# Order and time of the first loads of a convolution that runs beside an MLP: tap rows stored early, inputs in order of need

## Chip, cores, metric

One NeuronCore of one Trainium2 chip. Times are device microseconds (us) of one launch. Most executions of one kernel agree within 0.3%.

## The reference

Forward and backward of a block that adds two branches on a layer-normed input: a causal long convolution (with a short four-tap shift convolution of `k` ahead of it) and a gated MLP. Cut to what matters here:

```python
def _A_ref(q, k, v, shift_k, ssm_k, ssm_D):            # convolution branch
    k_shift = sum of four shifted copies of k, each times a column of shift_k
    kv = k_shift * v
    y = irfft(rfft(kv) * rfft(ssm_k)) + kv * ssm_D
    return q * y
def _B_ref(x, W_gate, W_up, W_down):                   # MLP branch
    h = relu(x @ W_gate) * (x @ W_up)
    return h @ W_down
return x + _A_ref(xn, ...) + _B_ref(xn, ...)           # and all gradients (vjp)
```

bf16, 2048 rows, width 1024, MLP width 3584. On the chip the convolution is done by small matmuls and VectorE transposes, in eight groups of 128 channels, threaded between the MLP's large matmuls.

## The kernel before

TensorE works through the MLP's first phase in groups of eight matmuls: two "gate" groups, two "up" groups, two "ps_h" groups, and so on. A generator `steps()` puts the convolution's work between them. A clock of the program counts 1730 per group; the convolution starts when it reaches `A_START`, and each `yield n` gives the MLP another n.

```python
    def loads_1(self, gi):                       # filter hn, gradient gt, bias sD
        ...
        for ch in range(2):
            self.load(hn[...], self.ssm_k[...])  # runs of 32 bf16 values
        self.load_time(gt, self.g, cg)           # two transfers
        self.load(sD[:], self.ssm_D[cg].partition_broadcast(P))
    def loads_2(self, st):                       # kp: four transfers; vt: two
        ...
    def load_taps(self, st):                     # tap rows, broadcast to 128 partitions
        skb = st["skb"] = self.sm.tile([P, 4, 1, P], BF16, name="skb")
        self.load(skb..., self.sk_d[4 * gi:4 * gi + 4, :]...partition_broadcast(P))
    def steps(self):
        sk_t = self.shift_rows()                 # transpose on TensorE, copy on ScalarE
        self.pin = True
        nx = self.loads_1(0)                     # hn, gt, sD
        self.loads_2(nx)                         # kp, vt
        yield 5000
        self.load(self.sk_d, sk_t[:])            # tap rows stored to DRAM
        yield 5000
        self.load_taps(nx)                       # ... and loaded again as skb
        yield 7000
        self.load_xn(nx)
        ...
        self.begin(nx)                           # first tap product: ksh = kp * skb
A_START = 80_000
```

All these transfers, and the MLP's stores and weight loads, are issued by SyncE, one after the other. VectorE carries the convolution's tap products and transposes and also empties the MLP's PSUM tiles (`ru <- ru, ps_u`); the MLP has four PSUM tiles (`bufs=4`).

## Time and profile before

| kernel before | |
|---|---|
| median, first runs | 1915.82 us (1914.72 to 1916.49) |
| profiled execution | 1911.9 us on the core, 1913.69 us as timed |
| TensorE busy | 1879.4 us of it |
| VectorE's longest wait near the start of the convolution | 8.29 us, on skb |
| TensorE's waits there | 3.21 and 1.67 us |
| TensorE's clock just after the first wait | 0.50 |

Read it from the engine that sets the end: TensorE is busy nearly always, so a microsecond is gained only where TensorE stands or runs at a lowered clock. The lines of the profile are in the prediction. One caution: the trace of before holds 15217 matmul records. Some are missing, and the many "issue" waits of 0.2 us are the holes that they leave. The busy share (98% before) must not be read as an effect.

### The profile page before, as it was taken

How to read it: one execution, taken by the hardware profiler on the slowest of the kernel's cores; microseconds unless marked ns; L12 is line 12 of the kernel's file. 1: busy time of each engine (PE TensorE's matmuls, PEld its weight loads, DVE VectorE, ACT ScalarE, POOL GpSimd, SP SyncE). 2: the span in 40 equal slices, each digit the busy share in tenths (PEclk: the TensorE clock that was granted, in tenths of full speed). 3: DMA queues.
4: the chain of work that ended last, by engine and by line, in shares of the span. 5: the costliest groups of instructions: out<-in, count | busy, mean ns of one | idle time of the engine just before them, and what ended most of it. 6: DMA issues, size and time to landing. Idle time of an engine off the chain costs nothing.

```text
span 1911.9 us, 35799 instructions
## 1 busy us (share of the span) xinstructions
PE 1879.4 (98%) x15217; PEld 872.8 (46%) x15447; DVE 909.8 (48%) x1355; ACT 618.3 (32%) x858; POOL 15.0 (1%) x37
## 2 busy tenths in 40 slices
PE   9989999999999999999999999999999999999999
PEld 4434444444444444444444444444444544444444
DVE  6656777777777764553454454400222232222222
ACT  5645345345345445344344354321000000000000
POOL 1000000000000000000000000000000000000000
PEclk9999999999999999999999999999999999999999
DMA  9887679977577774566563633394999965544553
GB/s 251 249 187 167 154 198 195 201 199 167 135 202 154 218 221 112 141 149 208 133 168 99 171 100 124 104 283 143 254 248 243 230 153 121 122 122 121 121 122 72
DMA packets 692641, 323.14 MB, mean 169 GB/s; under 512 B 524024, under 2 KB 663040, under 8 KB 692480
## 3 DMA queue, kind: packets, MB, share of 16 engines
q1 hardware_dynamic: 681984, 299.99, 63.5%
q10 hardware_dynamic: 9216, 16.65, 2.9%
q0 software_dynamic: 1280, 4.20, 0.6%
q8 instruction: 120, 1.97, 0.4%
q14 instruction: 41, 0.34, 0.1%
HBM read 143.79 MB, written 95.44 MB: 125 GB/s over the span
## 4 chain that ended last, share of the span: by engine, by line
PE 95%; DMA 2%; issue 1%; SPq 1%; DVE 1%; ACT 0%; DVEq 0%
PE ps_x L1319 20%; PE ps_w L1092 19%; PE ps_o L1250 10%; PE ps_u L835 9%; PE ps_h L835 9%; PE ps_g L835 9%; PE ps_d L1092 9%; PE ps L72 6%; PE ps_d L1105 1%; SPq L88 1%; PE ps_w L1105 1%; DMA wu<-in_B_W_up_dram 1%; DMA wg<-in_B_W_gate_dram 1%; PE ps_r L1280 0%; DVE flp L302 0%
## 5 line engine op out<-in xcount | busy, mean ns | idle before, releaser
L1092 PE MATMUL ps_w<-ugs,xn_nat 128*128 128x512 bf16 x1673 | 375.5, 379 | 5.7 <-issue 4.1
L835 PEld LDWEIGHTS <-xnT 128*128 128x128 bf16 x1792 | 170.9, 98 | 216.4 <-issue 17.6
L1092 PEld LDWEIGHTS <-xn_nat 128*128 128x128 bf16 x1728 | 164.5, 98 | 200.6 <-issue 7.6
L835 PE MATMUL ps_g<-wg,xnT 128*128 128x512 bf16 x869 | 205.2, 382 | 6.9 <-DVE ru L939 3.2
L835 PE MATMUL ps_u<-wu,xnT 128*128 128x512 bf16 x869 | 205.5, 381 | 3.0 <-issue 1.3
L835 PE MATMUL ps_h<-wdT,goT 128*128 128x512 bf16 x861 | 202.1, 379 | 2.6 <-issue 1.3
L1337 ACT ACTIVATE w<-xn,m 128x512 f32<-128x512 bf16 x32 | 24.3, 807 | 553.0 <-issue 317.2
L1319 PE MATMUL ps_x<-wuT,guT 128*128 128x512 bf16 x878 | 197.5, 379 | 1.0
L1319 PE MATMUL ps_x<-wgT,ggT 128*128 128x512 bf16 x878 | 197.3, 379 | 0.9
L1250 PE MATMUL ps_o<-wd,hT 128*128 128x512 bf16 (+1 forms) x879 | 186.7, 372 | 0.9
L1092 PE MATMUL ps_d<-g_nat,hs 128*128 128x512 bf16 x741 | 167.4, 379 | 3.2 <-issue 2.7
L1319 PEld LDWEIGHTS <-guT 128*128 128x128 bf16 x896 | 87.7, 98 | 105.7
L1319 PEld LDWEIGHTS <-ggT 128*128 128x128 bf16 x896 | 87.6, 98 | 105.5
L302 DVE STREAM_TRANSPOSE flp<-C 128x1024 f32<-128x1024 f32 x48 | 90.1, 1930 | 91.9 <-ACT C L76 91.9
L1250 PEld LDWEIGHTS <-hT 128*128 128x128 bf16 x896 | 87.7, 98 | 100.0
L835 PEld LDWEIGHTS <-goT 128*128 128x128 bf16 x896 | 84.9, 98 | 104.6 <-issue 5.7
L939 DVE SCALAR_TENSOR_TENSOR ru<-ru,ps_u 128x512 bf16<-128x512 bf16 x112 | 76.5, 683 | 107.8 <-issue 45.2
L1008 ACT CAST gh<-ps_h 128x512 bf16<-128x512 f32 x112 | 65.4, 584 | 172.3 <-PE ps_h L835 162.0
L1196 ACT CAST wi<-ps_w 128x512 bf16<-128x512 f32 x108 | 63.7, 590 | 162.9 <-PE ps_w L1092 154.0
L76 ACT CAST C<-ps 128x1024 bf16<-128x1024 f32 x96 | 92.5, 1015 | 71.0 <-PE ps L72 69.8
L1092 PEld LDWEIGHTS <-hs 128*128 128x128 bf16 x768 | 72.3, 98 | 89.6 <-issue 5.9
L1321 DVE CUSTOM_DVE_ANT_0 gx<-ps_x,gy 128x512 f32<-128x512 f32 x32 | 22.1, 691 | 187.1 <-PE ps_x L1319 185.1
(160 smaller groups left out, 1495.3 us busy)
## 6 DMA issues: line engine op xcount, KB each, us to landing
ug_d<-ru SPq DMA_DIRECT2D x112, 256.0 KB, 3.1
ugs<-ug_d SPq DMA_DIRECT2D x112, 256.0 KB, 5.3
wg<-in_B_W_gate_dram SPq DMA_DIRECT2D x56, 256.0 KB, 4.1
wu<-in_B_W_up_dram SPq DMA_DIRECT2D x56, 256.0 KB, 5.2
h_d<-ht SPq DMA_DIRECT2D x112, 128.0 KB, 2.4
hs<-h_d SPq DMA_DIRECT2D x56, 256.0 KB, 5.2
out_dram<-wi SPq DMA_DIRECT2D x56, 256.0 KB, 2.3
gt<-in_grad_out_dram SPq DMA_DIRECT2D x32, 256.0 KB, 4.0
```

The lines of the kernel that those rows point to most:

```text
L72: self.pri.pin(self.nc.tensor.matmul(out, lhsT=lhsT, rhs=rhs, start=start, stop=stop))
L76: self.pri.pin(self.nc.scalar.copy(out=out, in_=in_))
L302: self.pri.pin(self.nc.vector.transpose(out=df[:, c0:c0 + 32, :], in_=sf[:, c0:c0 + 32, :]))
L835: self.pri.pin(self.nc.tensor.matmul(ps[:], lhsT=xT[:, kt * P:(kt + 1) * P], rhs=w(kt), start=(kt == 0), stop=(kt == self.DT - 1)), always ...
L939: self.pri.pin(nc.vector.scalar_tensor_tensor(out=ru[s][:, 1, :], in0=ru[s][:, 0, :], scalar=0.0, in1=ps[:], op0=ALU.is_gt, op1=ALU.mult))
L1008: self.pri.pin(nc.scalar.copy(out=gh[:], in_=ps[:]))
L1092: self.pri.pin(self.nc.tensor.matmul(ps[:], lhsT=lhsT(st), rhs=rhs(st), start=(st == 0), stop=(st == self.ST - 1)))
L1105: self.pri.pin(self.nc.tensor.matmul(ps[i][:], lhsT=lhsT(i, st), rhs=rhs(i, st), start=(st == 0), stop=(st == self.ST - 1)))
L1196: self.pri.pin(nc.scalar.copy(out=wo[0][:, d, :], in_=ps[:]))
L1250: nc.tensor.matmul(ps, lhsT=hT[:, kt, :], rhs=self.wd[:, kt, oc], start=(kt == 0), stop=(kt == self.FT - 1))
L1319: nc.tensor.matmul(ps, lhsT=T[:, kt, :], rhs=W[:, kt, oc], start=(i == 0), stop=(i == n - 1))
L1337: nc.scalar.activation(out=w[:, oc], in_=xn[:, oc], func=ACT.Identity, scale=m[:, 7:8], bias=m[:, 6:7])
```

## The change

Its intent: the tap rows are made, stored and thus ready long before the convolution starts, and the first group's inputs are loaded in the order in which they are needed, with the MLP's stores let in between. The arithmetic starts at the same place (97,000 on the program's clock in both). Core of the diff:

```diff
-        nx = self.loads_1(0)
-        self.loads_2(nx)
-        yield 5000
+        yield 10000
         self.load(self.sk_d, sk_t[:])
-        yield 5000
+        yield 25000
+        nx = self.load_filter(0)      # hn
+        yield 3400
+        self.load_k(nx)               # kp
         self.load_taps(nx)            # skb
-        yield 7000
+        yield 3400
+        self.load_g(nx)               # gt, sD
+        yield 3400
+        self.load_v(nx)               # vt
+        yield 6800
         self.load_xn(nx)
...
-A_START = 80_000
+A_START = 45_000
```

(cut: `loads_1` and `loads_2` are split into `load_filter`, `load_g`, `load_k`, `load_v`; the other groups call them in the old order.)

More of the change, by code (lines that the diff above doesn't have):

```diff
@@ L245, in ttile, with load_filter @@
         return self.ts.tile([P, 19, P], BF16, name=name, tag="ts")
-    def loads_1(self, gi):
+    def load_filter(self, gi):
         cg = slice(gi * P, (gi + 1) * P)
@@ L252, in loads_1, with load_g @@
             self.load(hn[64 * ch:64 * ch + 64], self.ssm_k[c0:c0 + 64, :].rearrange("c (q n) -> q c n", n=NB1))
-        gt = self.ld.tile([P, 16, P], BF16, name="gt")
-        self.load_time(gt, self.g, cg)
-        sD = self.sm.tile([P, P], BF16, name="sD")
-        self.load(sD[:], self.ssm_D[cg].partition_broadcast(P))
-        return dict(gi=gi, cg=cg, hn=hn, gt=gt, sD=sD)
+        return dict(gi=gi, cg=cg, hn=hn)
+    def load_g(self, st):
+        gt = st["gt"] = self.ld.tile([P, 16, P], BF16, name="gt")
+        self.load_time(gt, self.g, st["cg"])
+        sD = st["sD"] = self.sm.tile([P, P], BF16, name="sD")
+        self.load(sD[:], self.ssm_D[st["cg"]].partition_broadcast(P))
+    def loads_1(self, gi):
+        st = self.load_filter(gi)
+        self.load_g(st)
+        return st
     def load_xn(self, st):
@@ L264, in gate_grad, with load_k, load_v, loads_2 @@
         self.tt(st["gt"][:], st["gt"][:], st["xt"][:], ALU.mult)
-    def loads_2(self, st):
-        nc, cg = self.nc, st["cg"]
-        kp = self.lng.tile([P, 19, P], BF16, name="kp")
+    def load_k(self, st):
+        nc = self.nc
+        kp = st["kp"] = self.lng.tile([P, 19, P], BF16, name="kp")
         self.pri.now()
         nc.gpsimd.memset(kp[0:1, 0:3, :], 0.0)
-        kv = self.tview(self.k, cg)
-        self.load_time(kp[:, 3:19, :], self.k, cg)
+        kv = self.tview(self.k, st["cg"])
+        self.load_time(kp[:, 3:19, :], self.k, st["cg"])
         self.load(kp[64:P, 0:3, :], kv[0, :, 13:16, :])
         self.load(kp[1:64, 0:3, :], kv[1, 0:63, 13:16, :])
-        vt = self.lng.tile([P, 16, P], BF16, name="vt")
-        self.load_time(vt, self.v, cg)
-        st["kp"], st["vt"] = kp, vt
+    def load_v(self, st):
+        vt = st["vt"] = self.lng.tile([P, 16, P], BF16, name="vt")
+        self.load_time(vt, self.v, st["cg"])
+    def loads_2(self, st):
+        self.load_k(st)
+        self.load_v(st)
     def load_taps(self, st):
```

## The prediction

> **What bounds the kernel now.** I read the page first: busy shares and the chain that ended last.
>
> ```profile
> PE 1879.4 (98%) x15217; PEld 872.8 (46%) x15447; DVE 909.8 (48%) x1355; ACT 618.3 (32%) x858; POOL 15.0 (1%) x37
> ...
> PE 95%; DMA 2%; issue 1%; SPq 1%; DVE 1%; ACT 0%; DVEq 0%
> ```
>
> TensorE carries the run: busy 98% of 1911.9 us, and 95% of the last chain. A change that only moves loads and one small store can gain no more than TensorE loses to waiting and to a lowered clock at the place concerned. So the second view is TensorE's waits over the whole span (us in total, times, longest):
>
> ```profile
> PE ps_w L1092 <- issue: 4.1, 26, 0.2
> PE ps_g L835 <- DVE ru L939: 3.2, 1, 3.2
> ...
> PE ps L72 <- DVE flp L302: 1.7, 1, 1.7
> ```
>
> Two single waits stand out, 3.2 us on VectorE's evacuation of an "up" product and 1.7 us on a VectorE transpose of the convolution. All others are 1.5 us or less, or many waits of 0.2 us. The third view, TensorE in order of time (start, duration), puts both in one place, just where the convolution branch begins:
>
> ```profile
> 115.62 3.63 PE L835 MATMUL ps_h<-wdT,goT 128*128 128x512 bf16 x15
> 119.08 1.89 PE L835 MATMUL ps_g<-wg,xnT 128*128 128x512 bf16 x8
> 124.18 3.57 PE L835 MATMUL ps_g<-wg,xnT 128*128 128x512 bf16 x8 [3.21 <-DVE ru L939]
> 127.55 4.79 PE L835 MATMUL ps_u<-wu,xnT 128*128 128x512 bf16 x16
> 132.17 1.89 PE L835 MATMUL ps_h<-wdT,goT 128*128 128x512 bf16 x7
> 135.73 0.75 PE L72 MATMUL ps<-flp,FW 64*32 64x128 bf16 x64 [1.67 <-DVE flp L302]
> ```
>
> The first line is the yardstick: two groups of eight matmuls from 115.62 to 119.08, 1.73 us a group. After the 3.21 us gap one group takes 3.37 us from start to start and the next two 4.62 instead of 3.46. The view by stretches shows why (the granted clock is the third number from the end, then come the DMA share and GB/s):
>
> ```profile
> 121.00:124.20 3.20, 0.02 (x1) 0.02 (x1) 1.86 (x3) 0.60 (x1) 0.00 (x0) 0.83 1.17 178
> 124.20:127.50 3.30, 3.30 (x8) 1.11 (x8) 3.26 (x6) 0.00 (x0) 0.00 (x0) 0.50 1.12 237
> 127.50:132.00 4.50, 4.50 (x17) 1.81 (x16) 4.47 (x5) 0.60 (x1) 0.00 (x0) 0.73 0.62 177
> ```
>
> The granted clock is 0.50 just after the gap and 0.73 on average over the next 4.5 us. TensorE counts as busy here, so the busy share hides this loss. The last view is VectorE in order of time, then the queue of SyncE, which issues the transfers:
>
> ```profile
> 113.59 0.43 DVE L941 TENSOR_TENSOR ht<-ru 128x512 bf16<-128x512 bf16 x1
> 122.31 1.23 DVE L80 TENSOR_TENSOR ksh<-kp,skb 128x2048 bf16<-128x2048 bf16 x1 [8.29 <-DMA skb<-sk_d]
> 123.45 0.68 DVE L939 SCALAR_TENSOR_TENSOR ru<-ru,ps_u 128x512 bf16<-128x512 bf16 x1
> ```
> ```profile
> 99.43 4.78 SPq L88 DMA_DIRECT2D hn<-in_A_ssm_k_dram  x2
> ...
> 113.69 1.31 SPq L88 DMA_DIRECT2D vt<-in_A_v_dram  x2
> 115.10 0.71 SPq L1013 DMA_DIRECT2D ug_d<-ru  x1
> 115.91 0.56 SPq L88 DMA_DIRECT2D sk_d<-sk_t  x1
> ...
> 119.13 0.33 SPq L88 DMA_DIRECT2D skb<-sk_d  x1
> ```
>
> VectorE stands 8.29 us before the first tap product, which needs the broadcast tap row skb. Behind it in VectorE's queue waits the evacuation of an up group that TensorE had finished at about 115.15. The MLP has four PSUM buffers; that unread group, two ps_h groups and one ps_g group fill them, so the second gate group can't start at 120.81 and starts at 124.18, as the evacuation at 123.45 ends. And skb is late because the burst of first-group inputs holds SyncE from 99.43 to 115.00: the row copy sk_t was ready at 96.0 (ScalarE's copy began at 95.76 and took 0.25), its store was issued only at 115.91, its load at 119.13, and skb was there at 122.31.
>
> **What the Trainium skill says.**
> - "PSUM — Partial Sum Buffer", Engine vs sequencer instructions: the queues of VectorE and ScalarE are strict FIFO. The trace agrees: the evacuation, ready at 115.15, ran 1.14 us after the tap product began, not before.
> - "TensorE: Matmul & The Clock Gate", Part 1: an idle window of about 3.4 us halves TensorE's clock, about 3.4 us of sustained work restores it, and a 512-column matmul then takes 426.7 ns start to start rather than 215.7. The trace agrees closely: 3.37 us for 8 is 421 ns, against 1.73 / 8 = 216 ns; a gap of 3.21 us was enough.
> - "DMA: Bandwidth & Descriptors", Anatomy of one DMA: a semaphore wait of a transfer is spent on the issuing sequencer, before dispatch. So a load that reads a just-stored tensor holds the queue behind it. The trace has 0.9 us of such a wait of SyncE on sk_d; most of the delay was the queue itself.
> - The same page, Why small descriptors are slow: a fixed overhead per packet. Filter hn goes in runs of 64 bytes (32 bf16 values); its stretch from about 104 to 105.5 shows the 16 DMA engines full at some 145 GB/s, so hn is the dear input.
>
> **The change, part by part.** Nothing is taken away: same loads, same store, same arithmetic.
>
> 1. Start and length of the preamble: before 80,000 + 5,000 + 5,000 + 7,000 = 97,000 on the program's step clock; after 45,000 + 10,000 + 25,000 + 3,400 x 3 + 6,800 = 97,000. The convolution's arithmetic enters at the same place between the MLP's matmuls.
>
> 2. Tap rows: the transpose (0.23 us on TensorE) and its copy (0.25 us on ScalarE) move some 35 us earlier, and the store of 8 KB some 45 us or more earlier, to about 75 us, when SyncE has room. Cost unchanged. The wait for this store drops out of skb's path.
>
> 3. skb: now directly after kp. hn keeps its place (issue 99.43 to 104.2). kp follows two steps (3.4 us) later, with one or two stores between: about 105 to 110 (4.52 us of issue in the old trace, an upper figure, since it queued behind hn). Then skb, 0.33 us, and 122.31 - 119.13 = 3.2 us to landing: about 113.5. VectorE is free for the tap product at 114.02. The 8.29 us wait should be gone or down to one or two.
>
> 4. What TensorE gains. The old walk against full speed, start to start: first gate group 5.10 instead of 1.73, lost 3.37 (the gap); second gate group 3.37, lost 1.64; two up groups 4.62 instead of 3.46, lost 1.16; ps_h group 3.56 instead of 1.73, lost 1.83 (the transpose). Sum **8.0 us**. At full speed TensorE comes to the flp matmuls at 119.08 + 5 x 1.73 = 127.73, not 135.73.
>
> 5. What VectorE then allows. Its chain to the second transpose in the old trace ran with no gap after the stall. In the new one, tap product, evacuation, ht and second product end by about 117.5; then the first "ru x gh" product must wait for ScalarE's gh, ready at 117.56 + 0.58 = 118.14 as before. From that product's start to the end of the second transpose the old trace took 135.68 - 125.64 = 10.04 us, so at best the transpose ends at 118.18 + 10.04 = 128.2, and TensorE waits 0.5 us there. Gain left: **7.5 us**.
>
> 6. What the new order can give back. sD, needed by the bias addition right after that product (about 118.9), was third in line and is now after hn, kp, skb and gt. Adding the old issue times from 99.43: hn 4.78, kp 4.52, skb 0.33, gt 3.61, sD 1.17 is 14.4; with some 2 us of stores and one transposed weight load (1.40) it is issued at about 117 and lands near 120 if queues stay as full as before. They should be emptier, as the burst is spread, so I charge half of that 1.1 us delay, 0.6 us, all on the path since VectorE has no slack by step 5.
>
> Sum 7.5 - 0.6 = 6.9 us; the rest of the span has no other part in the change, so 1915.8 - 6.9 = **1908.9 us**, 0.36% less.
>
> **Rivals.**
> A. Another input takes skb's place. The DMA engines are full nearly throughout from 99 to 119 us, and kp comes behind hn; if kp, skb or sD land 3 us late, TensorE waits 2 to 3 us at the transpose, though with a shorter gap the clock should not fall. For it: the full engines. Against it: kp moves ahead of gt and sD, 4.8 us of issue. Time: 1910.5 to 1912.
> B. VectorE as the local bound: the stall only hides VectorE's backlog, and later hand-overs (the gate product, the next transposes) slip too. For it: VectorE runs with hardly a gap from 122.31 to 141.27. Against it: half of that is catching up, and it idles 3.75 us right after. Time: about 1911.
> C. Full gain, with the transpose in time and weight loads and stores no longer stuck behind the burst: 1907.5.
> D. The wait was hidden anyway, or the stores between the loads hold SyncE while they wait for VectorE (4.1 us at the longest in the old trace) and so delay kp as much as the burst delayed skb: 1914 to 1917. Against it: the last chain is nearly all TensorE, and later loads would have to have been the true limit.
>
> **Range and chances.** C and the main line together have most of the weight, A and B about a third, D little. Run to run the old kernel moved by under 2 us. Range 1906.8 to 1913. The whole loss at the place is 8.0 us, 0.4%, so over 2% (38 us) either way would need something I can't see: faster 0.005, same 0.985, slower 0.01.
>
> **What would show it.** Right: sk_d stored before 80 us; tap product ksh starting at 114 to 116 with no long wait on skb; no TensorE wait on ru L939; clock 1.00 in the stretch 120 to 132 us; flp matmuls at 127.7 to 130 us; later phases like the old ones, shifted by about 7 us. Wrong: a wait of ksh on kp or of the bias addition on sD over 2 us; a wait on flp above 1.67 us; the shift shrinking again at the next weight loads; a new gap before 115 us.

## The result

| | before | after |
|---|---|---|
| median of the same rounds | 1916.15 us (1914.72 to 1917.26, 4 runs) | 1906.98 us (1905.80 to 1908.47, 4 runs) |
| ratio, with 95% interval | | 0.9953 (0.9936 to 0.9970) |
| profiled span | 1911.9 us | 1904.1 us |

The gain is clear of noise, 9 us or 0.5%; against the 2% mark it is "same". The time is inside the predicted range, but only 0.2 us above its lower end of 1906.8.

Two of TensorE's longest waits in the whole run after the change (a third, of 1.5 us in two parts, is at the very start, in the layer norm, and is 0.2 us in r_after below); the wait on the evacuation of `ps_u` is gone, that on the transpose is down from 1.7 to 0.5 us:

```profile
PE ps_warm L899 <- POOL warm L896: 1.5, 1, 1.5
PE ps L72 <- DVE flp L314: 0.5, 1, 0.5
```

TensorE after, in order of time (start, duration; lines of the program have moved by 17, so L835 is now L852):

```profile
115.76 3.63 PE L852 MATMUL ps_h<-wdT,goT 128*128 128x512 bf16 x16
119.22 3.62 PE L852 MATMUL ps_g<-wg,xnT 128*128 128x512 bf16 x16
122.67 3.62 PE L852 MATMUL ps_u<-wu,xnT 128*128 128x512 bf16 x16
126.13 1.89 PE L852 MATMUL ps_h<-wdT,goT 128*128 128x512 bf16 x8
128.53 0.75 PE L72 MATMUL ps<-flp,FW 64*32 64x128 bf16 x64 [0.51 <-DVE flp L314]
```

From the start of the ps_h groups to the flp matmuls it was 135.73 - 115.62 = 20.11 us and is 128.53 - 115.76 = 12.77 us. I call this stretch the walk. It is 7.34 us shorter. The clock, in the view by stretches (third number from the end), stays at 1.00 where it was 0.83, 0.50 and 0.73:

```profile
121.00:124.20 3.20, 3.20 (x17) 1.43 (x16) 3.17 (x4) 1.19 (x2) 0.00 (x0) 1.00 1.17 226
124.20:127.50 3.30, 3.30 (x17) 1.53 (x16) 3.27 (x4) 0.00 (x0) 0.00 (x0) 1.00 1.18 240
127.50:132.00 4.50, 3.99 (x80) 1.91 (x79) 4.47 (x6) 3.10 (x4) 0.00 (x0) 1.00 0.71 189
```

VectorE after: the tap product waits 0.93 us for skb instead of 8.29, and everything behind it comes earlier.

```profile
115.08 1.23 DVE L80 TENSOR_TENSOR ksh<-kp,skb 128x2048 bf16<-128x2048 bf16 x1 [0.93 <-DMA skb<-sk_d]
...
118.42 0.69 DVE L1026 TENSOR_TENSOR ru<-ru,gh 128x1024 bf16<-128x1024 bf16 x1
...
126.55 1.93 DVE L314 STREAM_TRANSPOSE flp<-B 128x1024 f32<-128x1024 f32 x1
```

The queue of SyncE after: the store of the tap rows 49 us earlier, skb 7 us earlier, one MLP store (ug_d) let in behind hn.

```profile
66.68 0.55 SPq L88 DMA_DIRECT2D sk_d<-sk_t  x1
...
99.11 5.61 SPq L88 DMA_DIRECT2D hn<-in_A_ssm_k_dram  x2
104.81 2.52 SPq L1030 DMA_DIRECT2D ug_d<-ru  x1
107.38 4.59 SPq L88 DMA_DIRECT2D kp<-in_A_k_dram  x4
112.02 0.37 SPq L88 DMA_DIRECT2D skb<-sk_d  x1
```

I also compared the starts of the same-numbered VectorE evacuations in the two traces. The new kernel is 0.1 to 0.4 us late until 113 us, 7.2 us ahead from then until 230 us, and 7.8 us ahead at the end. So the place accounts for nearly all of it; another 0.6 us comes at weight loads near 240 and 390 us.

### The profile page after: what moved, and what is told of

Read it like the earlier page. It is cut to its first block, busy times and chain, and to the rows that moved or that the text cites. A ratio compares the mean times of both kernels' runs of the same rounds, so it can differ in the third digit from the quotient of the medians. Undisturbed runs are those within 1.5% of the kernel's fastest.

```text
span 1904.1 us, 36029 instructions
## 1 busy us (share of the span) xinstructions
PE 1895.0 (100%) x15447; PEld 871.9 (46%) x15447; DVE 910.1 (48%) x1355; ACT 618.2 (32%) x858; POOL 15.0 (1%) x37
## 4 chain that ended last, share of the span: by engine, by line
PE 97%; DVE 1%; DMA 1%; issue 0%; SPq 0%; ACT 0%; DVEq 0%; ACTq 0%
PE ps_x L1336 20%; PE ps_w L1109 20%; PE ps_o L1267 10%; PE ps_h L852 10%; PE ps_u L852 10%; PE ps_g L852 9%; PE ps_d L1109 9%; PE ps L72 6%; PE ps_d L1122 1%; PE ps_w L1122 1%; DMA wg<-in_B_W_gate_dram 0%; PE ps_r L1297 0%; DMA wu<-in_B_W_up_dram 0%; SPq L88 0%; DVE ru L956 0%
## 5 line engine op out<-in xcount | busy, mean ns | idle before, releaser
L1109 PE MATMUL ps_w<-ugs,xn_nat 128*128 128x512 bf16 x1728 | 383.3, 379 | 0.0
L852 PEld LDWEIGHTS <-xnT 128*128 128x128 bf16 x1792 | 170.3, 98 | 209.8 <-issue 9.1
L852 PE MATMUL ps_g<-wg,xnT 128*128 128x512 bf16 x896 | 206.3, 379 | 1.5 <-ACT xnT L887 0.4
L852 PE MATMUL ps_u<-wu,xnT 128*128 128x512 bf16 x896 | 206.9, 379 | 0.0
L852 PE MATMUL ps_h<-wdT,goT 128*128 128x512 bf16 x896 | 205.6, 379 | 0.0
L1109 PE MATMUL ps_d<-g_nat,hs 128*128 128x512 bf16 x768 | 172.1, 379 | 0.0
L1336 PEld LDWEIGHTS <-ggT 128*128 128x128 bf16 x896 | 87.7, 98 | 105.5
L852 PEld LDWEIGHTS <-goT 128*128 128x128 bf16 x896 | 85.0, 98 | 104.7 <-issue 5.8
```

The lines of the kernel that those rows point to most:

```text
L852: self.pri.pin(self.nc.tensor.matmul(ps[:], lhsT=xT[:, kt * P:(kt + 1) * P], rhs=w(kt), start=(kt == 0), stop=(kt == self.DT - 1)), always ...
L1109: self.pri.pin(self.nc.tensor.matmul(ps[:], lhsT=lhsT(st), rhs=rhs(st), start=(st == 0), stop=(st == self.ST - 1)))
L1336: nc.tensor.matmul(ps, lhsT=T[:, kt, :], rhs=W[:, kt, oc], start=(i == 0), stop=(i == n - 1))
```

## The experiments

Eleven kernels ran: seven built on the changed kernel, two on the kernel before, and these two again as they are. All gave right results. "Flp less ksh" is the time from the start of the first tap product to the flp matmuls. The ratio is against the kernel before, whose medians were 1915.48 us (first four rows), 1915.39 us (next four) and 1916.02 us (last three); the first two profiles lead the table.

| kernel | ksh starts | flp matmuls | flp less ksh | walk | median us | ratio (95% interval) |
|---|---|---|---|---|---|---|
| before, first profile | 122.31 | 135.73 | 13.42 | 20.11 | | 1 |
| after, first profile | 115.08 | 128.53 | 13.45 | 12.77 | 1906.98 | 0.9953 (0.9936 to 0.9970) |
| r_after | 115.42 | 128.87 | 13.45 | 12.73 | 1906.90 | 0.9957 (0.9944 to 0.9969) |
| e5_filler | 123.42 | 136.80 | 13.38 | 20.99 | 1916.78 | 1.0009 (0.9996 to 1.0023) |
| e1_store_early | 122.97 | 136.38 | 13.41 | 20.62 | 1914.60 | 0.9999 (0.9986 to 1.0012) |
| e4_burst | 114.82 | 128.43 | 13.61 | 12.67 | 1906.22 | 0.9955 (0.9942 to 0.9967) |
| e2_taps_first | 118.78 | 132.18 | 13.40 | 15.64 | 1910.67 | 0.9974 (0.9961 to 0.9988) |
| e3_store_late | 115.88 | 129.31 | 13.43 | 13.70 | 1908.65 | 0.9962 (0.9950 to 0.9975) |
| e6_skb_ahead | 115.77 | 129.20 | 13.43 | 13.43 | 1907.50 | 0.9958 (0.9943 to 0.9973) |
| e7_flip_sooner | 115.85 | 128.09 | 12.24 | 12.19 | 1907.33 | 0.9954 (0.9942 to 0.9967) |
| r_before | 123.74 | 137.15 | 13.41 | 21.06 | 1915.29 | 1.0002 (0.9987 to 1.0018) |
| e9_burst_flip | 114.69 | 128.15 | 13.46 | 12.19 | 1906.66 | 0.9951 (0.9939 to 0.9964) |
| e8_begin_later | 125.96 | 139.21 | 13.25 | (other order) | 1912.46 | 0.9976 (0.9964 to 0.9989) |

**My theory after the two traces:** the flp matmuls come when VectorE's chain from ksh to the second transpose is done, and ksh starts when its last input lands; so only the landing of skb (and kp) counts. Rivals: the lowered clock is a loss of its own; the hour of the store matters; the MLP's stores held behind the burst matter.

**r_after: the changed kernel again.**

> The changed kernel again, for its time beside the others of this call and to see which gains away from the place repeat. The walk is the time on TensorE from the start of the two ps_h groups (115.62 us before, 115.76 after) to the first flp matmuls (135.73, 128.53): 20.11 us before, 12.77 after. Expected: walk 12.7 to 12.9, time 7 to 9.5 us below the kernel before. In the first two traces the shift grew by another 0.65 us at weight loads near 240 and 390 us; if that is chance of the transfers it will be another value here.

Measured: walk 12.73, ratio 0.9957. The gain near 390 us came again, but at 530 us the kernel lost about 1 us at weight loads, so in this trace it ends 6.9 us ahead of before. What happens away from the place moves by a microsecond from run to run and isn't the change's.

**e5_filler: fill TensorE's gap, leave the rest as before.**

```diff
                 ru[s] = self.e2_tile("ru")
+                if n == 2 and s == 5:
+                    junk = self.fill_ps.tile([P, 2, 512], F32, name="ps_junk", tag="aps")
+                    for _ in range(15):
+                        matmul(junk[:, 0], lhsT=xT[s][:, 0:P], rhs=wg(0), start=True, stop=True)
                 ps = self.ps_tile("ps_g")
```

(cut: the matmul call is shortened, and one line that lends the filler a PSUM tile of the convolution is left out.)

> Kernel before with 15 idle-filling matmuls (15 x 0.216 = 3.24 us) between the first and the second gate group of that step, just where TensorE stood 3.21 us; their result is read by nobody. Loads, stores and VectorE unchanged. Theory of the prediction, in which the lowered clock is a loss of its own (1.64 + 1.16 us of the 8.0): the gap is filled, the clock stays at 1.00 and the flp matmuls come 2.8 us earlier, walk about 17.3. Rival, the VectorE chain: VectorE ran without a gap from 122.31 to 135.68, so the flp matmuls can't come sooner; TensorE gets to them earlier and waits 1.67 + 2.8 = 4.5 us there instead of 1.67; walk 20.1, time as before.

TensorE in order of time with the filler:

```profile
121.00 3.40 PE L934 MATMUL ps_junk<-wg,xnT 128*128 128x512 bf16 x15
125.30 1.89 PE L835 MATMUL ps_g<-wg,xnT 128*128 128x512 bf16 x8 [0.90 <-DVE ru L944]
127.02 3.62 PE L835 MATMUL ps_u<-wu,xnT 128*128 128x512 bf16 x16
130.47 1.89 PE L835 MATMUL ps_h<-wdT,goT 128*128 128x512 bf16 x8
136.80 1.05 PE L72 MATMUL ps<-flp,FW 64*32 64x128 bf16 x64 [4.44 <-DVE flp L302]
137.79 2.48 PE L835 MATMUL ps_h<-wdT,goT 128*128 128x512 bf16 x6
```

Up to the flp matmuls the clock held: eight gate matmuls take 127.02 - 125.30 = 1.72 us, not 3.37. Yet the flp matmuls came no sooner. The wait for the transpose grew from 1.67 to 4.44 us, flp less ksh is 13.38 as ever, and the time didn't fall. So up to the flp matmuls the lowered clock had cost nothing: it ran beside VectorE's backlog. But the filler did not do away with it. After the wait of 4.44 us the granted clock was 0.50 from 136.45 to 139.86 us (in the trace of before it was 1.00 there), and six ps_h matmuls took 2.48 us. By my estimate that is 1.5 us lost, half of the 3.06 us in which TensorE was at work. The whole time, 1.0009, contains this loss and a longer stall, so it does not show what a restored clock is worth; the unchanged flp less ksh does. The skb wait was 9.21 us here, 0.9 longer than in the first trace of before, which explains the walk of 20.99; the expected 20.1 took the wait for fixed.

**e1_store_early: only the store of the tap rows early; inputs in the old order and burst, skb behind them.**

```diff
         yield 25000
-        nx = self.load_filter(0)
-        ... (kp, skb, gt, sD, vt with yields between)
+        nx = self.loads_1(0)
+        self.loads_2(nx)
+        yield 10000
+        self.load_taps(nx)
+        yield 7000
```

> Changed kernel, but the first group's inputs in the old order and in one burst, and skb loaded at its old place behind them; only the transpose and the store of the tap rows stay early. Theory (the queue order is what made skb late): skb is issued at about 117.5 instead of 119.13 and lands at about 120.7, ksh begins 1.6 us earlier than before, and with 13.37 us from ksh to the end of the second transpose the walk is about 18.4: gain 1.7 us. Rival (the late store is the cause): ksh no longer waits more than 1 us, walk 12.8, gain 7.

VectorE and SyncE of this kernel:

```profile
122.97 1.22 DVE L80 TENSOR_TENSOR ksh<-kp,skb 128x2048 bf16<-128x2048 bf16 x1 [8.81 <-DMA skb<-sk_d]
```
```profile
118.09 0.60 SPq L88 DMA_DIRECT2D skb<-sk_d  x1
```

No gain at all: less than the 1.7 us I expected, and nothing of the rival's 7. skb is issued 1 us earlier than before but takes 122.97 - 118.09 = 4.9 us until VectorE can use it, where it took 3.2 us when SyncE had stood waiting for the store. My reading is that what had been issued ahead of it still had to move, whether SyncE waited or not. The packet records in the traces bear this out. Four stores of the MLP, 768 packets of 1024 bytes, were issued between the burst and skb. When skb was issued, 64 packets of this size had started here and 592 in the trace of before; the 768th of this size started at 120.12 and at 119.78 us, and skb was there 2.8 and 2.5 us after that. The early store by itself is worth nothing.

**e4_burst: new order, but no stores between.**

```diff
         nx = self.load_filter(0)
-        yield 3400
         self.load_k(nx)
         self.load_taps(nx)
-        yield 3400
         self.load_g(nx)
-        yield 3400
         self.load_v(nx)
-        yield 6800
+        yield 17000
```

> Changed kernel with the new order of need (hn, kp, skb, gt, sD, v) but in one burst, with no stores between. Theory (only skb and kp in time matter): skb is issued at about 110, ksh starts at about 114, walk 12.7 to 13, gain 7 to 9 as the changed kernel. Rival (the stores held behind the burst matter): buffers of ru or ht come free late, a new wait of 1 us or more, walk 14 or more.

Measured: ksh at 114.82, walk 12.67, ratio 0.9955: the whole gain. The stores between the loads, a part of the change, do nothing for the time here; if anything kp and skb come 0.3 us sooner without them. Flp less ksh is 13.61, the longest of all: ksh was so early that VectorE's chain then waited for the product with `gh`, as the prediction's fifth step has it.

**e2_taps_first: skb first of all, the others in the old order and burst.**

```diff
-        nx = self.load_filter(0)
-        ... (kp, skb, gt, sD, vt with yields between)
+        nx = dict(gi=0)
+        self.load_taps(nx)
+        nx.update(self.loads_1(0))
+        self.loads_2(nx)
+        yield 17000
```

> Changed kernel with skb loaded first of all, ahead of hn, and the other inputs in the old order (hn, gt, sD, kp, v) and one burst. So skb is out of the question and kp, issued last but one, is the last thing ksh needs. From the first runs: the flp matmuls start 13.4 us after ksh starts, in every kernel. Theory (order of need matters, kp takes skb's place): kp's issue ends near 114, its last piece lands at about 117 to 118, ksh starts there, walk 14.7 to 16, gain 4 to 6 us. Rival (skb alone mattered): ksh starts by 115, walk 12.7 to 13, full gain.

```profile
118.78 1.23 DVE L80 TENSOR_TENSOR ksh<-kp,skb 128x2048 bf16<-128x2048 bf16 x1 [3.84 <-DMA kp<-in_A_k_dram]
```

A little over half the gain. With skb out of the question, kp takes its place: ksh starts 2.24 us after the ps_h groups (116.54), in the changed kernel 0.68 us before them. TensorE had no gap on `ps_u` any more; it waited 3.4 us on the transpose and its clock stayed at 1.00. So both halves of "order of need" count: skb ahead, and kp ahead of gt and sD.

**e3_store_late: new order and spread, the store of the tap rows late.**

```diff
-A_START = 45_000
+A_START = 80_000
...
-        yield 10000
-        self.load(self.sk_d, sk_t[:])
-        yield 25000
         nx = self.load_filter(0)
         yield 3400
+        self.load(self.sk_d, sk_t[:])
         self.load_k(nx)
```

> Changed kernel with the transpose and the store of the tap rows back at their late time: the store is issued just before kp's loads, skb after them; all else as in the changed kernel. Theory (the place of skb in the queue is the cause, not the hour of the store): the store lands while kp's loads are being issued (over 4 us), skb is issued at about 112 to 113, ksh starts at 115 to 116, walk 12.7 to 13.7, gain 6 to 9. Rival (the early store is needed): SyncE stands some 3 us before skb, ksh starts at 118 or later, walk 16 or more.

Measured: skb issued at 112.65 with no wait ahead of it, ksh at 115.88, walk 13.70, ratio 0.9962. The walk just reaches the end of what I had expected, 0.9 us more than the changed kernel's; the store now sits in the queue ahead of kp (0.56 us at 108.76), which may be part of that. Nor is 0.9 us far from chance: e7_flip_sooner below has the loads of the changed kernel, and its ksh came 0.6 us later in the walk. So the early store is worth at most some 1 us, the order 6 us or more.

**e6_skb_ahead: new kernel, skb ahead of hn.**

```diff
-        yield 25000
+        yield 22000
+        nx = dict(gi=0)
+        self.load_taps(nx)
+        yield 3000
-        nx = self.load_filter(0)
+        nx.update(self.load_filter(0))
         yield 3400
         self.load_k(nx)
-        self.load_taps(nx)
```

> Changed kernel with skb loaded between its store and hn, so that only kp is left to wait for. Theory (in the changed kernel VectorE's chain starts at the first product with gh, 118.2 to 118.4, so the 0.9 us wait for skb costs next to nothing): ksh starts near 114, walk 12.5 to 12.8, no time clear of noise against the changed kernel. Rival: each us of ksh's wait costs a us; walk 11.9.

A miss. In this schedule a transposed weight load (1.32 us at 106.37) went ahead of kp, kp landed at 115.77 and ksh waited 1.60 us for it. Walk 13.43, 0.7 longer than the changed kernel's; the time can't tell them apart. It didn't test whether an earlier ksh would still gain; e4_burst and e9_burst_flip did.

**e7_flip_sooner: one tap operation of the first group moved behind the transposes on VectorE.**

```diff
             yield None, self.both(lambda: self.add_D(st), tk)
             yield None, tk
-            yield None, tk
+            if gi:
+                yield None, tk
...
             yield None, flH
             yield None, flH
+            yield None, tk
             yield None, tk
             yield f2H, tk
```

> Changed kernel with one of the seven tap operations of the first group (1.23 us) moved from before to behind the two transposes on VectorE. Theory (the remaining 0.5 us wait of TensorE is VectorE's chain): the wait is gone, walk 12.3, and nothing waits in its place. Rival: the displaced operation delays the gate product and a wait of 0.5 us or more comes at the gt matmuls. Either is below what the time can show (0.5 us of 1907), so the profile decides.

```profile
128.09 0.75 PE L72 MATMUL ps<-flp,FW 64*32 64x128 bf16 x64
```
```profile
123.23 3.71 DVE L314 STREAM_TRANSPOSE flp<-B 128x1024 f32<-128x1024 f32 x2
```

No wait is left on this line, although ksh came 0.6 us later in the walk (0.05 us before the ps_h groups' start instead of 0.68) than in the changed kernel, and no new one appeared at the gt matmuls. The 12.24 us of flp less ksh are no longer VectorE's chain: both transposes are done at 123.23 + 3.71 = 126.94 us, 1.15 us before TensorE, at its own pace, comes to the flp matmuls. The chain itself, from ksh to the end of the second transpose, is 11.09 us instead of 13.40 in the changed kernel (115.08 to 126.55 + 1.93): the moved operation is 1.2 us of that, and the evacuation with its product that ran between the two transposes there, and runs behind them here, about 1.1 us. 0.5 us is not to be seen in the time.

**r_before: the kernel before again.**

> The kernel before, unchanged, once more: a second profile of it, and a timing of the same kernel against itself. Expected: ratio 1.000 within 0.0015; ksh waits 8 to 9.5 us for skb (8.29 in the first profile, 8.81 and 9.21 in two kernels with the same burst), so the stall itself moves by up to 1 us from run to run; flp matmuls 13.4 us after ksh; walk 20 to 21.2.

```profile
123.74 1.23 DVE L80 TENSOR_TENSOR ksh<-kp,skb 128x2048 bf16<-128x2048 bf16 x1 [9.25 <-DMA skb<-sk_d]
```

The stall is not a constant: 9.25 us here, 8.29 in the first profile. The walk is 21.06, so against r_after the gain at the place is 8.3 us, against 7.3 between the first two profiles. Timed against itself the kernel gives 1.0002.

**e8_begin_later: kernel before, convolution's arithmetic 9 us later.**

```diff
-        yield 7000
+        yield 16000
         self.load_xn(nx)
```

> Kernel before, all loads and the store in their old order and burst, but the convolution's arithmetic begins 9,000 on the step clock (some 9 us) later, so that the late skb (landing at 122 to 123) is there when VectorE comes to ksh at about 123. Theory (only the gap between skb's landing and its first use costs time): ksh waits under 1.5 us, the clock stays at 1.00, and the MLP's later evacuations come 6 to 7.5 us sooner than before; the convolution ends 9 us later, at about 1255 us less the gain, well before its products are needed at 1328; time 6 to 9 us under before. Rival (the burst of loads costs by itself, by stores and weight loads held behind it): most of the loss stays, gain under 3 us.

```profile
125.96 1.23 DVE L80 TENSOR_TENSOR ksh<-kp,skb 128x2048 bf16<-128x2048 bf16 x1 [5.70 <-DMA skb<-sk_d]
```
```profile
245.96 3.34 PE L835 MATMUL ps_u<-wu,xnT 128*128 128x512 bf16 x8 [2.64 <-DMA wu<-in_B_W_up_dram]
```

Half right. There was no TensorE wait on the evacuation of `ps_u` and the clock stayed at 1.00, but skb landed 3 us later than I took it to, and ksh waited 5.70 us, not under 1.5. Flp less ksh is 13.25, and TensorE waited 1.75 us for the transpose. Part of the gain at the place was given back later: one weight load made TensorE wait 2.64 us, the granted clock was 0.50 from 247.02 to 250.43 us, and the eight matmuls after the wait, half of them at that clock, took 3.34 us instead of 1.9. The time fell by 0.24%, half of what the change gives. Where the remaining microsecond or two went I did not trace; shifting the convolution against the MLP moves all later meetings of transfers. It does not support the rival that the burst costs by itself, which e4_burst refutes more cleanly.

**e9_burst_flip: e4_burst and e7_flip_sooner together.** The edits are those two.

> The shortest walk that the runs point to: new order of need in one burst (ksh at 114.8 with it) and the transposes one tap operation sooner. Expected: no wait at the flp matmuls, walk 12.1 to 12.2, time 8 to 10 us under before; against the changed kernel about 0.6 us at the place, which the times can't separate.

Measured: walk 12.19 as expected, no wait at the flp matmuls, ratio 0.9951. Its walk is the shortest, with e7's, but the times can't tell it from the changed kernel: the intervals overlap almost wholly.

## Why the prediction was right

1. **What was bound by what.** Right. The 8.29 us of VectorE on skb were the source; with skb in time both waits of TensorE went, except for the 0.5 us that step 5 named. The walk through at full speed, 119.08 + 5 x 1.73, gave 127.73 for TensorE's arrival; e7, where nothing waits, shows 128.09 with a start 0.28 us later. One reading on the way does not hold: the four PSUM tiles were not all unread when the second gate group stood. ScalarE had read the two ps_h tiles by 118.14 and 119.87 us (`gh` at 117.56 and 119.28), and the group stood until 124.18. It waited for one tile, the `ps_u` tile that VectorE had not emptied; that the tiles are used strictly in turn is my inference.

2. **Start and tap rows (steps 1 and 2).** Right: arithmetic at the same place (0.14 us apart at 113 us); the store at 66.68 instead of "about 75".

3. **skb at 113.5 (step 3).** It landed at 115.08; VectorE waited 0.93 us. Inside the "one or two" allowed for. It cost almost nothing: VectorE would have stood before the product with `gh` anyway, which began at 118.42 against the predicted 118.18. In e4_burst ksh began 0.26 us earlier and the flp matmuls only 0.10.

4. **The sum of 8.0 us (step 4).** As an account of the old trace it stands, but its parts are not separate causes. e5_filler filled the gap and took away with it the 1.64 and 1.16 us of lowered clock, and the flp matmuls came no sooner. The cause is one number, the start of ksh: flp less ksh is 13.38 to 13.45 in every kernel in which ksh waited for a load by 0.88 us or more and VectorE's order was the old one (in e7, e8 and e9 it is another, and in e7 and e9 TensorE's own arrival sets the flp matmuls). The prediction escaped the mistake because step 5 took VectorE's chain, not the sum, as the limit.

5. **Gain left of 7.5 us (step 5).** Measured 7.34 between those two traces, with the 0.5 us of wait predicted.

6. **0.6 us for a late sD (step 6).** Wrong. sD was issued at 114.25, not 117, and the bias addition (119.02) waited for nothing: the two gt loads took 1.32 us to issue, not 3.61, and the transposed weight load came behind sD (119.64), not ahead of it. That the queue ahead had drained is my reading of the 1.32 us; no run tests it.

7. **Two readings beside the main line.** The stretch of hn in which the DMA engines moved some 145 GB/s runs from about 103.0 to 104.75 us and again from 106.5 to 107.4 us, not from 104 to 105.5; its packets are of 64 bytes, so hn was dear as said. And the clock agrees with the page only in the pace of the matmuls, not in what lowers and restores it (see the last section).

The prediction says 6.9 us; the medians say 9.2 us, and 8.6 us in r_after. The two profiled executions, 1913.69 and 1905.84 us, are 7.85 us apart. From 6.9 to there it is the sD term (0.6 us) and the gain near 240 and 390 us (0.6 us), less 0.2 us of step 5. The rest, 1.3 us on the medians, is a matter of the starting point: the profiled execution of before was 2.5 us under its median, that of after 1.1 us, and I took a loss read in that one execution off the median of the others. The old stall is not a constant (8.29 us in that execution, 9.25 in r_before, 9.21 in e5), and I took it for one; that this is most of the 1.3 us is not shown.

Of the rivals, A (another input takes skb's place) is what e2 shows for the old order, and didn't happen in the new one, though in e6_skb_ahead, close to it, ksh waited 1.60 us for kp. B (VectorE as a local bound) is true in its cause and small in its size, 0.5 us. C (full gain, 1907.5 us) is nearest to the measured time, but by chance: the transpose was not in time, the 0.5 us wait was there, and e4_burst, which lets no store through, gains as much. D is out.

## What to carry to other kernels

When an engine that empties PSUM also does other work in order, a late small load in front of that work can stop the matmuls; look for it behind the matmul engine's longest single wait, then follow the engine's queue back to the load and the load's queue back to what was issued ahead of it. What decided here was the place of a load in the issuing queue: put the loads in the order of first use. Making the source ready earlier gave at most 1 us here, and spreading the others out nothing. Don't add up a gap, a lowered clock and a later wait as three gains: if another engine runs without a gap from the first to the last, its chain is the only one. And before a loss read in a profile is taken off a median, see how far the profiled execution is from that median.

## What the Trainium skill lacked or had wrong

- "DMA: Bandwidth & Descriptors" (Anatomy of one DMA): its cost of a transfer, a fixed part of about 2 us and a part by bytes, is fitted to single transfers issued by GpSimd; those here are SyncE's. The same 128 KB broadcast load took 3.2 us from issue to use in the kernel before and 4.9 us in e1_store_early, where more of the stores ahead of it had still to move. The fit has no term for what is queued ahead.
- "TensorE: Matmul & The Clock Gate" (Part 1): one idle window of about 3.4 us halves the clock. Here a gap of 3.21 us was enough once, and two waits of 3.39 us (e2_taps_first) and 3.0 us (r_before, after its first) were not, so the length of the gap is no threshold. In e8_begin_later a wait of 2.64 us was enough, and the clock fell 1.06 us after its end; in the first trace of before it fell 2.1 us into the gap. By the clock records it stayed down for 3.41 us in four traces (e1, e5, e8, r_before) and for 6.83 us, twice that, in the first of before, where TensorE worked for 5.7 us (from 124.18 to 129.91) before it rose; the page has about 3.4 us of sustained work. Steps of 3.41 us fit the page's free-running window, and where that window lies may account for the 5.7 us; that a window has to be idle throughout does not fit the two falls just named.
- The same page counts the lowered clock as a loss. In e5_filler full clock up to the flp matmuls brought them no sooner (flp less ksh 13.38 us, 13.42 before), as VectorE set the pace; I found no page that says to check for that first.
- "PSUM — Partial Sum Buffer" (Engine vs sequencer instructions) has strict FIFO queues on VectorE, and every trace here agrees; that such a queue carries a wait for a load over to the matmuls (8.29 us there, 3.21 us on TensorE) stands on no page that I read.
